# Seven weight-tile subtractions moved from VectorE to GpSimd

## The chip, the core and the metric

The kernel runs on one core of one Trainium2 chip. The metric is the time of one execution on the device in microseconds (us). Engine names in the profile: PE is TensorE (matrix products; PEld its weight loads), DVE is VectorE, ACT is ScalarE, POOL is GpSimd, SP is the engine that issues most transfers.

## The reference

A delta-rule recurrence over 32 heads (4 x 8, 768 steps, head size 48), followed by a two-layer network with a clipped quadratic in the middle:

```python
for t in range(S):
    y[:, :, t] = np.einsum('bhd,bhde->bhe', q[:, :, t], state)
    v_old = np.einsum('bhde,bhd->bhe', state, kt)
    state = state + bt[..., None] * np.einsum('bhd,bhe->bhde', kt, vt - v_old)
...
h = x @ w_in                       # 3072 x 384 @ 384 x 2048
g = np.where(h >= 1, h, np.where(h <= -1, 0, (h + 1) ** 2 / 4))
out = g @ w_out                    # 3072 x 2048 @ 2048 x 384
```

All inputs are fp32.

## The kernel before

**Two computations in one.** The recurrence is done in chunks of 64 steps; two chunks make a group G of 512 rows for the network, six groups in all. For each chunk, Gram matrices are formed on TensorE and triangular systems are solved on VectorE (in the first two groups by L355 and L357, a product and a subtraction per step, called inversion steps here; later by L366 and L368), then merged and applied in a chain of small products.

**The network** runs in items. An item n is one tile f of 128 hidden columns for the rows of one group: `up` (L738, nine products into a PSUM bank h), an activation (L877), the square (L891), the clipping on VectorE (L893, called square(n) in the prediction; it reads h and is what frees it), a rounding to `ghi` on ScalarE (L856) and the rest `glo` on VectorE (L857), and `down` (L753), which follows two items later. There are two h banks, so up(n) waits for L893 of item n - 2. The items of the first group are six of half width, ten of full width (n = 6 to 15, tiles 6 to 15), then the other halves of the first six.

**Numbers in two parts.** Products run on a rounded high half and a low half, in three passes. The network's weights come as 16 tiles, each with both layers' part, as packed integers, and are unpacked once, in the first part of the run, in five steps per tile f:

```python
def grow(f):    # ScalarE, L189
def shift(f):   # VectorE, L195
def join(f):    # VectorE, L201
def cast(f):    # ScalarE, L205: high half, WT[f][:, :, 0, :]
def low(f):     # VectorE, L208: low half, WT[f][:, :, 1, :]
```

Steps on VectorE stand in the fixed order shift(f), join(f), low(f - 1); those on ScalarE in the order grow(f + 2), cast(f). The unpacked numbers lie in `X4` (`xb` in the profile), four slots taken in turn, so grow(f + 4) needs low(f). `up` and `down` of tile f need its low half.

**Order.** Every engine works its instructions in the order in which the program issues them. The order is written out by hand: the strings FILL give, for each item, which steps of unpacking (A for ScalarE, D for VectorE), of the solver, of loads and of masks stand at which place.

**Other work of VectorE around the place of the edit:** the masks of Q (L264, from PSUM), scalings of V (L292), transposes (L394, L396), subtractions from PSUM (L498). GpSimd clears parts of `XT` (L393, L449) there, and later masks Q (L272) and A (L331).

Of the kernel before, what the change touches and what calls it, by code (L numbers as in the profile page):

```python
# [11 lines left out]
ALU = mybir.AluOpType  # L12
# [28 lines left out]
def delta_rule_moe(ctx: ExitStack, tc: tile.TileContext, kqa, kqb, kv, beta, w, out):  # L41
# [14 lines left out]
    nc = tc.nc  # L56
# [14 lines left out]
    K, KE, GE, Q, KV, XB, RAW, WT = {}, {}, {}, {}, {}, {}, {}, {}  # L71
# [112 lines left out]
    X4 = sb.tile([P, 4, 2, DM], F32, name="xb")  # L184
# [20 lines left out]
        nc.scalar.copy(out=WT[f][:, :, 0, :], in_=X4[:, f % 4])  # L205

    def low(f):
        nc.vector.tensor_tensor(out=WT[f][:, :, 1, :], in0=X4[:, f % 4], in1=WT[f][:, :, 0, :], op=ALU.subtract)  # L208

    done = set()  # L210

# [447 lines left out]
    spare += START  # L659
    acts = [(f, grow) for f in range(2)] + [x for f in range(FT) for x in ((f + 2, grow), (f, cast)) if x[0] < FT]  # L660
    vecs = [x for f in range(FT + 1) for x in ((f, shift), (f, join), (f - 1, low)) if 0 <= x[0] < FT]
    sv, ln, raws = [scale_v(g) for g in range(4)], [lanes(0), lanes(1)], []
    tasks = {"A": unpack(acts), "D": unpack(vecs), "B": restore(), "L": ln[1], "s": sv[0], "t": sv[1], "v": sv[2], "z": sv[3]}
# [197 lines left out]
    for n, item in enumerate(items):  # L861
# [9 lines left out]
        if at_ == 2 * HALF:  # L871
            spare.clear()
        assert (item[1], low) in done, item
        h = up(*item)

# [74 lines left out]
```

## Time and profile before

| | |
|---|---|
| median of three runs | 591.88 us (589.80 to 596.24) |
| profiled execution | 590.3 us, of which the span of its instructions 588.6 us |
| busy in the span | PE 97%, PEld 84%, DVE 69%, ACT 56%, POOL 9% |
| granted TensorE clock, mean | 0.992 |

The shares are of the whole span, over stages that differ; the edit touches some 40 us of it.

### The profile page before, as it was taken

What the parts mean: (1) busy time and instruction counts of PE and PEld (TensorE: products, weight loads), DVE (VectorE), ACT (ScalarE), POOL (GpSimd) and SP (SyncE); (2) the same over time, 40 slices, a digit from 0 to 9 for tenths busy, and PEclk for the clock granted to TensorE, in tenths of its full rate; (3) what the DMA queues carried; (4) which work ended last, traced back from release to release, by engine and by line L of the source; (5) the groups of instructions that cost most, each with busy time, mean ns of one, the idle gap of its engine ahead of it and who ended that gap; (6) DMA issues with size and microseconds to landing.
All of it is one profiled execution on the core that took longest, in us unless ns stands there. A gap on an engine that the chain in (4) does not pass through costs nothing.

```text
span 588.6 us, 21697 instructions
## 1 busy us (share of the span) xinstructions
PE 569.0 (97%) x9585; PEld 493.3 (84%) x9585; DVE 405.2 (69%) x828; ACT 327.5 (56%) x587; POOL 54.5 (9%) x91
## 2 busy tenths in 40 slices
PE   8998899999999999999999999999999999999996
PEld 7776788788978888888888888888888888898986
DVE  5977999963689864599954599954599955333332
ACT  4648886358644575545575445575445564454443
POOL 6200010000000500010400011300011300000000
PEclk9979999999999999999999999999999999999999
DMA  5673766200333111134011134011133000020001
GB/s 147 199 253 138 213 212 192 77 4 10 95 81 100 31 32 39 39 97 114 24 33 41 37 103 119 16 30 45 36 106 96 1 3 16 15 55 1 0 2 53
DMA packets 32302, 42.77 MB, mean 73 GB/s; under 512 B 7056, under 2 KB 26768, under 8 KB 32208
## 3 DMA queue, kind: packets, MB, share of 16 engines
q1 hardware_dynamic: 31216, 40.41, 24.0%
q8 instruction: 75, 1.23, 0.9%
q0 software_dynamic: 576, 0.57, 0.4%
q10 hardware_dynamic: 416, 0.39, 0.2%
q14 instruction: 19, 0.16, 0.1%
HBM read 34.47 MB, written 4.72 MB: 67 GB/s over the span
## 4 chain that ended last, share of the span: by engine, by line
PE 47%; issue 22%; DVE 14%; DMA 6%; SPq 6%; ACT 2%; POOL 1%; POOLq 0%; DVEq 0%; ACTq 0%
PE h L738 18%; PE o L753 17%; DMA wt<-in_w_dram 4%; PE ch L534 3%; PE ch L237 2%; DVE s L893 2%; PE ch L508 2%; DVE pr L366 1%; DVE A L368 1%; DVE glo L857 1%; PE ch L250 1%; SPq L595 1%; PE ch L492 1%; DMA KV<-in_kv_dram 1%; DVE wt L208 1%
## 5 line engine op out<-in xcount | busy, mean ns | idle before, releaser
L738 PE MATMUL h<-xb,wt 128*128 128x512 f32 (+1 forms) x918 | 223.0, 386 | 5.1 <-DVE s L893 2.0
L753 PE MATMUL o<-wt,ghi 128*128 128x384 f32 x768 | 200.0, 342 | 0.1
L738 PEld LDWEIGHTS h<-xb,wt 128*128 128x128 f32 x918 | 161.8, 188 | 38.9 <-DVE s L893 3.4
L753 PEld LDWEIGHTS o<-wt,ghi 128*128 128x128 f32 x768 | 137.2, 188 | 7.0 <-issue 0.3
L753 PE MATMUL o<-wt,glo 128*128 128x384 f32 x384 | 129.4, 337 | 0.4 <-DVE glo L857 0.4
L856 ACT CAST ghi<-s 128x512 fp32r<-128x512 f32 (+1 forms) x102 | 60.8, 597 | 120.4 <-DVE s L893 107.8
L893 DVE SCALAR_TENSOR_TENSOR s<-s,h 128x512 f32<-128x512 f32 (+1 forms) x102 | 66.3, 650 | 77.1 <-ACT s L891 76.8
L877 ACT ACTIVATE s<-h,half 128x512 f32<-128x512 f32 (+1 forms) x102 | 67.4, 661 | 53.8 <-PE h L738 53.6
L857 DVE TENSOR_TENSOR glo<-s,ghi 128x512 fp32r<-128x512 f32 (+1 forms) x102 | 66.8, 654 | 39.5 <-ACT ghi L856 39.3
L753 PEld LDWEIGHTS o<-wt,glo 128*128 128x128 f32 x384 | 72.1, 188 | 1.0 <-DVE glo L857 1.0
L891 ACT ACTIVATE s<-s 128x512 f32<-128x512 f32 (+1 forms) x102 | 62.2, 610 | 2.2
L368 DVE TENSOR_TENSOR A<-A,pr 128x30 f32<-128x30 f32 (+14 forms) x120 | 45.4, 378 | 4.4
L366 DVE TENSOR_TENSOR pr<-A 128x30 f32<-128x30 f32 (+14 forms) x120 | 43.4, 362 | 2.2
L272 POOL TENSOR_SCALAR_AFFINE_SELECT Q<-Q 64x512 f32<-64x512 f32 x32 | 21.7, 680 | 117.4 <-ACT Q L260 116.0
L165 PE MATMUL o<-wx 128*128 128x512 f32 x87 | 27.8, 464 | 1.5 <-DVE tiny L175 1.5
L534 PEld LDWEIGHTS ch<-Q,SU 64*64 64x64 f32 (+3 forms) x1056 | 22.4, 135 | 3.7 <-ACT ghi L856 1.5
L534 PE MATMUL ch<-Q,SU 64*64 64x64 f32 (+3 forms) x1056 | 24.7, 222 | 0.0
L331 POOL TENSOR_SCALAR_AFFINE_SELECT A<-A 128x1024 f32<-128x1024 f32 x4 | 5.6, 1390 | 191.5 <-DMA xb<-X 148.1
L165 PEld LDWEIGHTS o<-wx 128*128 128x128 f32 x87 | 18.2, 220 | 5.6 <-DVE tiny L175 1.5
L626 DVE TENSOR_TENSOR SU<-ch,SU 48x384 f32<-48x384 f32 x36 | 19.9, 554 | 3.9 <-PE ch L607 3.5
L590 DVE TENSOR_TENSOR X<-ch,X 128x128 fp32r<-128x128 f32 x20 | 5.8, 292 | 23.5 <-ACT xb L586 22.5
L517 ACT COPY SU<-ch 64x384 f32<-64x384 f32 (+1 forms) x30 | 14.3, 476 | 7.0 <-PE ch L508 6.7
(168 smaller groups left out, 559.5 us busy)
## 6 DMA issues: line engine op xcount, KB each, us to landing
wt<-in_w_dram SPq DMA_DIRECT2D x16, 768.0 KB, 5.6
out_dram<-wx SPq DMA_DIRECT2D x44, 96.0 KB, 2.2
KV<-in_kv_dram SPq DMA_DIRECT2D x36, 96.0 KB, 2.4
KV<-in_kv_dram SPq DMA_DIRECT2D x72, 48.0 KB, 2.3
KV<-in_kv_dram SPq DMA_DIRECT2D x12, 192.0 KB, 2.7
xb<-X SPq DMA_DIRECT2D x60, 32.0 KB, 2.0
K<-in_kqb_dram SPq DMA_DIRECT2D x12, 128.0 KB, 2.6
Q<-in_kqb_dram SPq DMA_DIRECT2D x12, 128.0 KB, 2.7
```

Of the source, the lines that this page charges most:

```text
L165: nc.tensor.matmul(warm_ps, warm[:, 0:P], warm, start=True, stop=True)
L272: nc.gpsimd.affine_select(out=y, in_=y, pattern=[[0, H], [1, C]], base=0, channel_multiplier=-1, compare_op=ALU.is_gt, fill=0.0)
L366: nc.vector.tensor_tensor(out=pr, in0=A[:, 0:n, j:j + 1].broadcast_to([P, n, m]), in1=A[:, j:j + 1, j + 1:32].broadcast_to([P, n, m]), op= ...
L368: nc.vector.tensor_tensor(out=A[:, 0:n, j + 1:32], in0=A[:, 0:n, j + 1:32], in1=pr, op=ALU.add)
L534: nc.tensor.matmul(yy[i][o * C:o * C + C, e, p], SF[rows, u:u + C], w_[rows, x, k, :], **how)
L738: nc.tensor.matmul(h[:, cols(bs)], WT[f][:, 0, x, k * P:(k + 1) * P], XB[G][:, y, k, cols(bs)], start=(n == 0), stop=(n == 8))
L753: nc.tensor.matmul(oacc[G, k], (ghi, glo)[x][:, k * P:(k + 1) * P], WT[f][:, 1, y, :], start=(new and n == 0), stop=(left[G, b] == 0 and n ...
L856: nc.scalar.copy(out=ghi[:, c], in_=s[:, c])
L857: nc.vector.tensor_tensor(out=glo[:, c], in0=s[:, c], in1=ghi[:, c], op=ALU.subtract)
L877: nc.scalar.activation(out=s[:, c], in_=h[:, c], func=AF.Relu, bias=mid, scale=0.5)
L891: nc.scalar.activation(out=s[:, c], in_=s[:, c], func=AF.Square)
L893: nc.vector.scalar_tensor_tensor(out=s[:, c], in0=s[:, c], scalar=1.0, in1=h[:, c], op0=ALU.min, op1=ALU.max)
```

## The change

For tiles 9 to 15 the subtraction low(f) is issued to GpSimd in place of VectorE. Operands, place in the program and everything else stay as they are.

```diff
     def low(f):
-        nc.vector.tensor_tensor(out=WT[f][:, :, 1, :], in0=X4[:, f % 4], in1=WT[f][:, :, 0, :], op=ALU.subtract)
+        (nc.gpsimd if f > 8 else nc.vector).tensor_tensor(out=WT[f][:, :, 1, :], in0=X4[:, f % 4], in1=WT[f][:, :, 0, :], op=ALU.subtract)
```

On GpSimd, in the stretch from the transfers of staged rows (L595) to the clearing of `XT` (L449), the seven subtractions stand as follows (`xb_176` is X4, `wt9` to `wt15` the weight tiles):

```order
 L314 MEMSET X_619 128x16 x2
 L595 DMA xb_865<-wt15_1416 16x2x256 x3
+L208 TENSOR_TENSOR wt9_1617<-xb_176,wt9_1617 128x2x384
+L208 TENSOR_TENSOR wt10_1650<-xb_176,wt10_1650 128x2x384
+L208 TENSOR_TENSOR wt11_1740<-xb_176,wt11_1740 128x2x384
 L393 MEMSET XT_173 128x32x16
+L208 TENSOR_TENSOR wt12_1788<-xb_176,wt12_1788 128x2x384
+L208 TENSOR_TENSOR wt13_1883<-xb_176,wt13_1883 128x2x384
+L208 TENSOR_TENSOR wt14_1993<-xb_176,wt14_1993 128x2x384
+L208 TENSOR_TENSOR wt15_2242<-xb_176,wt15_2242 128x2x384
 L449 MEMSET XT_173 32x16x32 x4
```

The memset of L393 now stands behind three subtractions and those of L449 behind all seven.

On VectorE, where tile 10 is joined and tile 9's low half was made, ahead of two inversion steps:

```order
 L201 SCALAR_TENSOR_TENSOR xb_176<-wt10_1398,xb_176 128x768
 L857 TENSOR_TENSOR glo_1621<-s_1602,ghi_1620 128x512
-L208 TENSOR_TENSOR wt9_1617<-xb_176,wt9_1617 128x2x384
 L355 TENSOR_TENSOR pr_1625<-X_619,A16_712 128x126
 L357 TENSOR_TENSOR X_619<-X_619,pr_1625 128x2x7x9
```

The inversion steps follow `glo` at once.

On VectorE, where tile 13 is joined and tile 12's low half was made, ahead of tile 14's shift and join:

```order
 L201 SCALAR_TENSOR_TENSOR xb_176<-wt13_1555,xb_176 128x768
 L893 SCALAR_TENSOR_TENSOR s_1821<-s_1821,h_1811 128x512
-L208 TENSOR_TENSOR wt12_1788<-xb_176,wt12_1788 128x2x384
 L195 TENSOR_SCALAR xb_176<-xb_176 128x768
 L201 SCALAR_TENSOR_TENSOR xb_176<-wt14_1615,xb_176 128x768
```

Shift and join of tile 14 follow the clipping at once. TensorE, ScalarE and SP have the same instructions in the same order as before.

## Rows read from the trace of the kernel before

**Rows 1.** Page, part 1: busy us, share of span, instructions.

```profile
PE 569.0 (97%) x9585; PEld 493.3 (84%) x9585; DVE 405.2 (69%) x828; ACT 327.5 (56%) x587; POOL 54.5 (9%) x91
```

**Rows 2.** Windows: busy us by engine, clock, DMA share, GB/s.

```profile
88.00:116.30 28.30, 26.26 (x609) 22.28 (x608) 27.75 (x54) 14.20 (x22) 0.50 (x1) 1.00 0.47 139
...
127.10:588.60 461.50, 453.79 (x6819) 398.19 (x6818) 296.60 (x602) 249.45 (x451) 36.67 (x50) 1.00 0.18 47
```

**Rows 3.** Waits of PE and PEld, 76 to 131: total, times, longest.

```profile
PE h L738 <- DVE s L893: 2.0, 3, 1.1
...
PEld h L738 <- DVE wt L208: 0.6, 1, 0.6
...
PEld o L753 <- DVE glo L857: 0.3, 1, 0.3
```

**Rows 4.** Timeline of DVE, 70 to 132: start, us, instruction.

```profile
85.10 0.68 DVE L893 SCALAR_TENSOR_TENSOR s<-s,h 128x512 f32<-128x512 f32 x1
85.70 0.95 DVE L201 SCALAR_TENSOR_TENSOR xb<-wt,xb 128x768 int32<-128x768 int32 x1
...
87.17 0.95 DVE L208 TENSOR_TENSOR wt<-xb,wt 128x768 fp32r<-128x768 f32 x1
88.03 0.29 DVE L355 TENSOR_TENSOR pr<-X,A 128x126 f32<-128x126 f32 x1
...
92.15 2.09 DVE L264 TENSOR_TENSOR Q<-ch,mask 64x512 f32<-64x512 f32 x3
...
101.51 0.22 DVE L355 TENSOR_TENSOR pr<-X,A 128x56 f32<-128x56 f32 x1
...
109.36 0.96 DVE L201 SCALAR_TENSOR_TENSOR xb<-wt,xb 128x768 int32<-128x768 int32 x1
...
110.69 1.22 DVE L394 STREAM_TRANSPOSE XT<-A 128x512 f32<-128x512 f32 x1
111.81 0.64 DVE L857 TENSOR_TENSOR glo<-s,ghi 128x512 fp32r<-128x512 f32 x1
```

**Rows 5.** Timeline of ACT, 70 to 132: casts of tiles 9 and 10.

```profile
84.47 0.83 ACT L205 CAST wt<-xb 128x768 fp32r<-128x768 f32 x1
...
88.45 0.82 ACT L205 CAST wt<-xb 128x768 fp32r<-128x768 f32 x1
```

**Rows 6.** Timeline of POOL, whole span (idle before, releaser in brackets).

```profile
3.83 0.81 POOL L148 TENSOR_SCALAR_AFFINE_SELECT perm<-perm 128x32 f32<-128x32 f32 x3
...
115.80 1.09 POOL L449 MEMSET XT<- 32x512 f32 x2 [36.29 <-PE ch L419]
...
164.50 1.26 POOL L331 TENSOR_SCALAR_AFFINE_SELECT A<-A 128x1024 f32<-128x1024 f32 x1 [43.45 <-PE ch L607]
...
191.18 3.12 POOL L272 TENSOR_SCALAR_AFFINE_SELECT Q<-Q 64x512 f32<-64x512 f32 x4 [25.19 <-ACT Q L260]
...
285.99 2.89 POOL L272 TENSOR_SCALAR_AFFINE_SELECT Q<-Q 64x512 f32<-64x512 f32 x4 [4.69 <-ACT Q L260]
```

**Rows 7.** Timeline of DVE beside two of these maskings.

```profile
192.86 0.68 DVE L893 SCALAR_TENSOR_TENSOR s<-s,h 128x512 f32<-128x512 f32 x1
...
286.82 0.68 DVE L368 TENSOR_TENSOR A<-A,pr 128x58 f32<-128x58 f32 x1
...
288.23 0.71 DVE L368 TENSOR_TENSOR A<-A,pr 128x30 f32<-128x30 f32 x1
```

**Rows 8.** Timeline of DVE, 254 to 256.5, GpSimd idle.

```profile
255.68 0.19 DVE L368 TENSOR_TENSOR A<-A,pr 128x30 f32<-128x30 f32 x1
...
256.15 0.22 DVE L368 TENSOR_TENSOR A<-A,pr 128x58 f32<-128x58 f32 x1
```

**Rows 9.** Timeline of PE, 70 to 140: a merge, up(13), a chain product.

```profile
114.44 1.26 PE L419 MATMUL ch<-A,XT 32*32 32x16 f32 x128
...
116.35 2.36 PE L738 MATMUL h<-xb,wt 128*128 128x512 f32 x9 [0.65 <-DVE s L893]
...
136.90 1.36 PE L508 MATMUL ch<-KV,XT 64*64 64x48 f32 x64
```

## Prediction

> **What bounds the kernel now.** I read the busy shares first, then windows by stretch, the waits of TensorE, and last the timelines of VectorE, ScalarE and GpSimd where the seven subtractions lie. VectorE is busy for 405.2 us of the span and GpSimd for 54.5 [rows 1]; as averages these two shares invite the move. They hide that the edit touches one stretch only. From 88.0 to 116.3 us VectorE is busy for 27.75 of 28.30 us and TensorE is the engine with holes, 26.26 us; from 127.1 us to the end TensorE is busy for 453.79 of 461.50 us and VectorE for little more than half [rows 2]. In the first of these stretches TensorE's waits are VectorE's doing: 2.0 us in three waits of `up` for the L893 that frees its h bank, 0.6 us of a weight load for a low half itself (L208), 0.3 us for a `glo` [rows 3]. Together 2.9 us: no relief of VectorE can give back more than about that. One of the three waits stands ahead of `up(13)`, 0.65 us [rows 9].
>
> Names below: low(f), join(f) (L201), shift(f) (L195) and cast(f) (L205) are the steps of tile f; glo(n) (L857), square(n) (L893), up(n) and down(n) belong to item n. In the stretch of the edit item n uses tile n.
>
> **What leaves VectorE.** Seven subtractions of 0.95 us; the next instruction starts 0.87 us after one (88.03 after 87.17) [rows 4], so 7 x 0.87 = 6.1 us. Of these, five (tiles 9 to 13) lie ahead of square(11), the last that TensorE waits for; the other two lie where VectorE already idles for ScalarE, so they are worth nothing on the path. Without any other effect, 5 x 0.87 = 4.4 us earlier at square(11) is more than TensorE can take: the three waits for L893 go whole, 2.0 us, and of the 0.9 us for a low half and a `glo` about half, which overlaps them. I count 2.4 us; then there is no gap left.
>
> **What it costs on GpSimd.** No two-input operation of GpSimd is in the trace, so its length is bounded by rows. The one-input select on 128x1024 took 1.26 us and three on 128x32 took 0.81, or 0.27 each [rows 6]: 1.0 ns per element over 0.27, hence 1.04 us for 768 elements if a second input were free. If it costs as much as the first, 0.27 + 2 x 0.77 = 1.81 us. The dearest row per element is the masking of Q, 3.12 us for four of 512, 1.5 ns per element, which doubled gives 2.3 us. I take 1.8 us, since the 128x1024 row is the nearest in partitions and length; the ends are 1.04 and 2.3.
>
> GpSimd itself has room: each tile's subtraction becomes ready with its cast on ScalarE, 84.47 to 85.30 us for tile 9 [rows 5], where VectorE came to it only at 87.17. So the low halves are finished no later than before, and the 0.6 us weight-load wait goes. Two sorts of GpSimd memsets now stand behind subtractions in its queue. The one of L393 comes behind low(11), about 95 us, and the first product that reads its zeros (L419) runs from 114.44 [rows 9]. The four of L449, which began at 115.80 [rows 6], come behind low(15), about 125 us; four of some 0.55 us end near 128, ahead of the product L508 at 136.90 [rows 9]. Both cost nothing while GpSimd keeps within some 8 us of that.
>
> **The lock.** The decisive row is what happens to VectorE beside GpSimd. While GpSimd masked Q (four selects in 2.89 us, 0.72 each) [rows 6], VectorE's inversion steps of 58 and 30 elements (L368), with both inputs in SBUF, took 0.68 and 0.71 us [rows 7]; the same shapes alone took 0.22 and 0.19 [rows 8]. Each waited about 0.5 us, until GpSimd's instruction was nearly through. An L893 in the middle of such a masking (192.86, within 191.18 to 194.30), with one input in PSUM, took 0.68, no more than elsewhere [rows 4, 6, 7]. So VectorE stands still for about the length of a GpSimd instruction less 0.2, whenever its next instruction has two SBUF inputs, and goes on where one input is PSUM. In SBUF - State Buffer, section "Who interferes with whom", the Trainium skill gives this as an exclusive lock, taken by a VectorE instruction with two SBUF inputs or in a two-port mode against a GpSimd one that reads SBUF; the trace agrees.
>
> Shift(f) has its one input and its output in SBUF, and no row shows one beside GpSimd; I take it as held, and where it is not the waits of low(10) and low(13) below are 0.3 us shorter each. Joins, inversion steps (L355, L357), `glo` and scalings of V are of the held kind by rows 7; the squares, the masks of Q from PSUM (2.09 us at 92.15), the transposes (L394) and the subtractions from PSUM are not. I price the hold at 1.7 us: 1.81, less 0.2, plus some 0.1 for starting again.
>
> **Following the order with a hold of 1.7 us.**
> - low(9): cast(9) is done at 85.30, VectorE is in square(6) from 85.10 [rows 4, 5]. GpSimd starts at about 85.37, and join(10), due at 85.70, waits until 87.07: 1.37 us.
> - low(10): cast(10) ends near 89.2 [rows 5], VectorE is in shift(11), whose end near 89.54 lets GpSimd in until 91.24. Square(7) runs beside it for 0.60, then join(11) waits 1.10 us.
> - low(11): it gets in as the mask of Q begins (2.0 us from PSUM), and is through when that is: 0.
> - low(12): inversion steps and scalings follow without a gap (L355 at 101.51 is one) [rows 4]: the whole 1.70 us.
> - low(13): shift(14) ends, join(14) (109.36) waits 1.70 us.
> - low(14): the transpose L394 (110.69) covers part; glo(10) (111.81) waits 1.03 us.
>
> Together 6.9 us of waits ahead of glo(10). Taken away ahead of it are four subtractions, 3.5 us. So glo(10) ends 3.4 us later, and down(10), which waited for it by 0.3 us already, stands 3.3 us later. Square(11) comes behind low(13) too, so it is 3.4 - 0.9 = 2.5 us later. TensorE loses the 0.65 us gap that it had ahead of up(13): 3.3 - 0.65 = **2.6 us later**. From there VectorE is ahead again, and the rest of the run is TensorE's at 98% busy, with nothing in it that takes 2.6 us back. low(15) falls where VectorE waits for ScalarE.
>
> **Sum.** The profiled execution took 590.3 us (588.6 span, 1.7 around it); 590.3 + 2.6 = 592.9. The median of the three runs is 591.9, 1.6 above it; on that the forecast is **594.5 us**, plus 0.4%.
>
> **Rivals.**
> 1. No hold: VectorE and GpSimd run side by side in this pairing. Then the 2.4 us above are gained: 591.9 - 2.4 = 589.5. For it: holds are seen with selects and with products only. Against: the held rows have two inputs in SBUF, as the joins have, and the new instruction reads twice what a select reads.
> 2. Slower by a cascade: the GpSimd instruction holds for 1.9 us or more. From about 1.85 the order turns: low(10) is ready before VectorE has begun shift(11) and holds that too, join(11) and cast(11) come later, low(11) misses the cover of the mask multiplication, and shift(12) waits for it. At 1.9 the same following gives 4.9 us at up(13), at 2.3 it gives 7.3: 596.8 to 599.2. For it: 1.81 is only 0.1 off that point. Against: the waits in rows 7 were shorter than the GpSimd instruction, not longer.
> 3. The second input is nearly free: a hold of 1.04 us. The waits ahead of square(11) are then 3.9 us against 4.4 removed; the time stays within 0.5 us of 591.9. For it: the 1.0 ns per element of L331. Against: it would have to read two tensors at the pace of one.
>
> GPSIMD Engine Reference of the Trainium skill, section "Performance versus the Vector engine", gives 4497 ns for a two-input add of 2048 elements, as an estimate 1.7 us pro rata for 768; no run here shows it, and the sum by it would be the forecast. By its advice to keep elementwise work on VectorE the sign would be the forecast's too.
>
> That the edit does not do what it says can be left out: the order shows seven instructions gone from VectorE and seven on GpSimd, and nothing else moved.
>
> **How the numbers follow.** Forecast, hold between 1.4 and 1.85 us (1.2 to 3.2 us slower): 0.55. Rival 2: 0.25. Rival 1: 0.12. Rival 3: 0.08. About 1% (5.9 us) is what a measurement of this kernel can tell from no change. Only the dearer half of rival 2 is beyond it, holds over some 2.1 us, 0.16, with 0.03 for a hold priced wrongly in kind: slower 0.19. Faster by 1% is not to be had from 2.9 us of waits: 0.03. Within: 0.78. The range reaches from rival 1, 589.0, to rival 2's end, 599.5.
>
> **What would show it.** In the changed kernel's timeline GpSimd has seven L208 of 1.7 to 2.0 us, the first near 85.4. VectorE's join(10), join(11), an inversion step near 101, join(14) and glo(10) are 1 to 1.7 us longer than alone, squares and the masks from PSUM keep theirs. VectorE's busy time hardly falls, since waits count as busy. TensorE's wait ahead of up(10) grows, down(10) waits some 3 us for `glo`, and up(13) starts near 119 in place of 116.35. I am wrong if joins keep 0.95 us beside a GpSimd L208 (rival 1), if those last over 2 us or under 1.3, if VectorE gets in front of a waiting GpSimd instruction so that low(12) comes late for up(12), or if a later stage takes the delay back.

## The result and the profile after

The changed kernel takes 594.89 us (median of 20 runs, 591.95 to 599.18), the kernel before 590.93 us (20 runs, 588.79 to 596.24). The ratio of the runs is 1.0063, 95% interval 1.0044 to 1.0081: by it the change costs 3.7 us, 2.6 to 4.8. The profiled execution took 594.9 us, its span 593.2.

The page's first part [rows 1] reads now:

```profile
PE 571.5 (96%) x9585; PEld 495.0 (83%) x9585; DVE 405.8 (68%) x821; ACT 328.3 (55%) x587; POOL 67.7 (11%) x98
```

VectorE has seven instructions less and is busy for as long as before; GpSimd has 13.2 us more. The windows around the edit [rows 2]:

```profile
88.00:119.00 31.00, 25.90 (x508) 22.19 (x503) 29.77 (x49) 14.14 (x24) 9.97 (x6) 0.94 0.40 120
119.00:130.00 11.00, 11.00 (x350) 9.18 (x340) 6.85 (x12) 4.71 (x9) 3.94 (x5) 1.00 0.06 14
130.00:593.00 463.00, 454.13 (x6825) 398.32 (x6819) 296.27 (x602) 250.13 (x451) 36.75 (x50) 1.00 0.18 47
```

TensorE has some 5 us of holes between 88 and 119 us, where it had 2 in the 28 us from 88 to 116.3, and the last number but two, its granted clock, is 0.94 there. GpSimd's timeline shows the seven subtractions (start, us, what ended the idle time before):

```profile
84.26 1.85 POOL L208 TENSOR_TENSOR wt<-xb,wt 128x768 fp32r<-128x768 f32 x1 [6.44 <-ACT wt L205]
88.19 2.05 POOL L208 TENSOR_TENSOR wt<-xb,wt 128x768 fp32r<-128x768 f32 x1 [2.09 <-PE ch L250]
92.55 1.87 POOL L208 TENSOR_TENSOR wt<-xb,wt 128x768 fp32r<-128x768 f32 x1 [2.32 <-ACT wt L205]
94.36 0.53 POOL L393 MEMSET XT<- 128x512 f32 x1
99.97 1.92 POOL L208 TENSOR_TENSOR wt<-xb,wt 128x768 fp32r<-128x768 f32 x1 [5.08 <-ACT wt L205]
108.85 1.85 POOL L208 TENSOR_TENSOR wt<-xb,wt 128x768 fp32r<-128x768 f32 x1 [6.96 <-ACT wt L205]
112.46 1.81 POOL L208 TENSOR_TENSOR wt<-xb,wt 128x768 fp32r<-128x768 f32 x1 [1.76 <-ACT wt L205]
123.36 1.86 POOL L208 TENSOR_TENSOR wt<-xb,wt 128x768 fp32r<-128x768 f32 x1 [9.09 <-ACT wt L205]
125.29 2.24 POOL L449 MEMSET XT<- 32x512 f32 x4
```

And VectorE's timeline, the instructions that lay beside them [rows 4]:

```profile
83.94 0.68 DVE L893 SCALAR_TENSOR_TENSOR s<-s,h 128x512 f32<-128x512 f32 x1
84.53 2.39 DVE L201 SCALAR_TENSOR_TENSOR xb<-wt,xb 128x768 int32<-128x768 int32 x1
...
89.03 2.02 DVE L201 SCALAR_TENSOR_TENSOR xb<-wt,xb 128x768 int32<-128x768 int32 x1
...
92.63 2.09 DVE L264 TENSOR_TENSOR Q<-ch,mask 64x512 f32<-64x512 f32 x3
94.63 0.67 DVE L195 TENSOR_SCALAR xb<-xb 128x768 int32<-128x768 int32 x1
...
100.20 1.78 DVE L357 TENSOR_TENSOR X<-X,pr 128x78 f32<-128x78 f32 x1
...
109.01 2.51 DVE L201 SCALAR_TENSOR_TENSOR xb<-wt,xb 128x768 int32<-128x768 int32 x1
...
113.01 1.81 DVE L857 TENSOR_TENSOR glo<-s,ghi 128x512 fp32r<-128x512 f32 x1
```

Two more lengths of the kernel before, from its timeline of VectorE (a shift and an inversion step of 78 elements):

```profile
88.56 0.55 DVE L195 TENSOR_SCALAR xb<-xb 128x768 int32<-128x768 int32 x1
...
101.23 0.24 DVE L357 TENSOR_TENSOR X<-X,pr 128x78 f32<-128x78 f32 x1
```

The joins take 2.39, 2.02 and 2.51 us in place of 0.95 or 0.96, the inversion step 1.78 in place of 0.24, the `glo` of item 10 1.81 in place of 0.64. Their waits add up to 1.44 + 1.07 + 1.54 + 1.55 + 1.17 = 6.8 us, 6.9 with 0.12 us of shift(12), which took 0.67 beside the memset of L393. Squares and the mask of Q keep their length beside the same GpSimd instructions.

TensorE's timeline from down(10) to up(13) [rows 9], and its clock in windows:

```profile
112.04 0.62 PE L753 MATMUL o<-wt,ghi 128*128 128x384 f32 x2
114.88 0.45 PE L753 MATMUL o<-wt,glo 128*128 128x384 f32 x1 [2.21 <-DVE glo L857]
115.16 0.73 PE L753 MATMUL o<-wt,ghi 128*128 128x384 f32 x2
...
118.06 1.49 PE L419 MATMUL ch<-A,XT 32*32 32x16 f32 x128
```

```profile
114.00:116.00 2.00, 1.12 (x4) 1.12 (x5) 2.00 (x3) 0.00 (x0) 0.28 (x1) 0.82 0.00 0
116.00:118.00 2.00, 2.00 (x7) 1.63 (x6) 1.76 (x3) 0.17 (x1) 0.00 (x0) 0.50 0.32 97
118.00:120.00 2.00, 2.00 (x131) 1.87 (x131) 0.83 (x2) 1.83 (x4) 0.00 (x0) 0.83 0.51 121
```

TensorE stands for 2.21 us for glo(10), and right behind it its granted clock is 0.50, half of 2.4 GHz, for some 3.4 us.

Executions differ by some microseconds ahead of this place: square(6) starts at 85.10 before and at 83.94 after, though no instruction ahead of it was changed. So the stretch from the start of square(6) to the start of up(15) is the measure of the edit in a trace. It is 45.82 us before (130.92 less 85.10) and 50.10 after (134.04 less 83.94): 4.28 us longer. From TensorE's timelines, before and then after:

```profile
130.92 2.37 PE L738 MATMUL h<-xb,wt 128*128 128x512 f32 x9
```

```profile
134.04 2.36 PE L738 MATMUL h<-xb,wt 128*128 128x512 f32 x9
```

### The profile page after: what moved, and what is told of

It reads as the page before. It is cut to its first block, busy times and chain, and to the rows that moved or that the text cites. A ratio compares the mean times of both kernels' runs of the same rounds, so it can differ in the third digit from the quotient of the medians.

```text
span 593.2 us, 21710 instructions
## 1 busy us (share of the span) xinstructions
PE 571.5 (96%) x9585; PEld 495.0 (83%) x9585; DVE 405.8 (68%) x821; ACT 328.3 (55%) x587; POOL 67.7 (11%) x98
## 4 chain that ended last, share of the span: by engine, by line
PE 49%; issue 22%; DVE 13%; DMA 7%; SPq 4%; ACT 3%; POOL 1%; POOLq 0%; DVEq 0%; ACTq 0%
PE h L738 19%; PE o L753 17%; DMA wt<-in_w_dram 4%; PE ch L534 3%; PE ch L237 2%; PE ch L508 1%; DVE glo L857 1%; DVE xb L201 1%; DVE A L368 1%; DVE pr L366 1%; PE ch L250 1%; DVE s L893 1%; PE ch L492 1%; DMA xb<-X 1%; DMA KV<-in_kv_dram 1%
## 5 line engine op out<-in xcount | busy, mean ns | idle before, releaser
L165 PE MATMUL o<-wx 128*128 128x512 f32 x87 | 29.0, 479 | 1.5 <-DVE tiny L175 1.5
L201 DVE SCALAR_TENSOR_TENSOR xb<-wt,xb 128x768 int32<-128x768 int32 x16 | 19.3, 1206 | 0.1
```

The source lines that it names most:

```text
L165: nc.tensor.matmul(warm_ps, warm[:, 0:P], warm, start=True, stop=True)
L201: nc.vector.scalar_tensor_tensor(out=x, in0=RAW.pop(f).bitcast(I32)[:, :, 0::2], scalar=29, in1=x, op0=ALU.logical_shift_right, op1=ALU.bi ...
```

## The experiments

Theory 1 is that of the forecast: a GpSimd instruction that reads SBUF holds any VectorE instruction with two inputs there. Theory 2: VectorE is not held, TensorE waits for late low halves. Theory 3: any GpSimd work beside VectorE slows it. Experiments 1 to 6 are edits of `low(f)` of the kernel before, 9 of that and of one memset; 7 and 8 start from the changed kernel. L208 stays L208 in all of them.

| kernel | ratio to before, 95% interval | square(6) to up(15), us | against before |
|---|---|---|---|
| before | 1 | 45.82 | |
| changed | 1.0063 (1.0044 to 1.0081) | 50.10 | +4.28 |
| 1 memset in place | 0.9957 (0.9929 to 0.9985) | 42.94 | -2.88 |
| 2 subtraction in addition | 1.0157 (1.0118 to 1.0196) | 54.52 | +8.70 |
| 3 memsets in addition | 1.0033 (1.0003 to 1.0064) | 46.74 | +0.92 |
| 4 tiles 13, 14 | 1.0102 (1.0053 to 1.0150) | 51.11 | +5.29 |
| 5 tiles 9 to 12 | 1.0044 (1.0007 to 1.0082) | 47.92 | +2.10 |
| 6 tiles 10, 12, covered | 0.9998 (0.9966 to 1.0030) | 44.55 | -1.27 |
| 7 changed, wait filled | 1.0087 (1.0057 to 1.0118) | 49.50 | +3.68 |
| 8 changed again | 1.0090 (1.0053 to 1.0128) | 48.04 | +2.22 |
| 9 covered, memset ahead | 0.9980 (0.9948 to 1.0011) | 43.85 | -1.97 |

The stretch is one execution each; the ratios rest on 4 to 20 runs of the kernel in the row.

**1. An instruction that only writes, in place of the subtraction.**

```diff
-        nc.vector.tensor_tensor(out=WT[f][:, :, 1, :], ...)
+        nc.gpsimd.memset(WT[f].bitcast(F32)[:, :, 1, :], 0.0) if f > 8 else nc.vector.tensor_tensor(...)
```

> For tiles 9 to 15 GpSimd fills the low half with zeros in place of subtracting: an instruction that only writes. The low halves of these seven tiles are left out, all else is as in the changed kernel. Theory 1 (VectorE is held by a GpSimd instruction that reads SBUF, whenever its own has two inputs there): the joins keep 0.95 us, VectorE is relieved of seven subtractions and nothing is charged, so 2.0 to 2.4 us faster than before, ratio 0.996. Theory 2 (the loss comes from late low halves, VectorE itself is not held): also faster, since zeros come early, but then the wait ahead of down(10) in the changed kernel would have to be for a low half. Theory 3 (any GpSimd work beside VectorE slows it): no gain, ratio 1.000 or above.

Measured: 0.9957, the stretch 2.88 us shorter. The gain that the forecast gave to a world without holds is there as soon as GpSimd reads nothing. VectorE's own subtraction in this kernel, beside the first memset (84.41 to 85.15 us on GpSimd), and an inversion step of 126 elements beside the second (87.72 to 88.46) take what they take in the kernel before [rows 4]:

```profile
84.72 0.95 DVE L208 TENSOR_TENSOR wt<-xb,wt 128x768 fp32r<-128x768 f32 x1
...
88.13 0.28 DVE L355 TENSOR_TENSOR pr<-X,A 128x126 f32<-128x126 f32 x1
```

Theory 3 falls here for work with two inputs. Theory 2 has no support in the changed kernel's trace, where nothing waits for a low half.

**2. The subtraction in addition.**

```diff
+    scratch = sb.tile([P, 2, DM], F32, name="wx")
     def low(f):
         nc.vector.tensor_tensor(out=WT[f][:, :, 1, :], ...)
+        f > 8 and nc.gpsimd.tensor_tensor(out=scratch, in0=X4[:, f % 4], in1=WT[f][:, :, 0, :], op=ALU.subtract)
```

> VectorE makes all low halves as before; GpSimd does the seven subtractions in addition, into a tile that nobody reads. Theory 1: the waits of the changed kernel without its relief, so glo(10) and square(11) are some 7 to 8 us late: 6.5 to 9 us slower than before, ratio 1.011 to 1.015. Theory 2 (late low halves): the low halves come from VectorE at their old place, so no change, ratio 1.000. Theory 3: as theory 1.

Measured: 1.0157, a little above the range, which its interval covers; the stretch is 8.70 us longer. No low half that is used comes from GpSimd here, so theory 2 falls; holds without relief cost about what theory 1 said: glo(10) ends 8.25 us later, counted from square(6), where 7 to 8 were expected. VectorE's timeline:

```profile
87.92 2.41 DVE L201 SCALAR_TENSOR_TENSOR xb<-wt,xb 128x768 int32<-128x768 int32 x1
...
91.72 1.93 DVE L355 TENSOR_TENSOR pr<-X,A 128x126 f32<-128x126 f32 x1
...
99.49 1.67 DVE L208 TENSOR_TENSOR wt<-xb,wt 128x768 fp32r<-128x768 f32 x1
```

A join, an inversion step and VectorE's own subtraction wait 1.46, 1.64 and 0.72 us; with a scaling of V, join(14) and glo(10), not shown here, it is 8.2 us. GpSimd can wait as well: its fifth subtraction here is recorded for 2.63 us, behind a subtraction and a shift of VectorE.

**3. Memsets in addition.** After each cast GpSimd copies one element and clears the unused tile three times, 2.3 us.

```diff
+        f > 8 and [nc.gpsimd.tensor_copy(out=scratch[:, 0, 0:1], in_=WT[f][:, 0, 0, 0:1])] + [nc.gpsimd.memset(scratch, 0.0) for _ in range(3)]
```

> VectorE makes all low halves as before; for each of tiles 9 to 15 GpSimd, after the cast, copies one element and then clears a tile that nobody reads three times, over 2 us of writing. Theory 1: instructions that only write do not hold two-input work; the fast one-input shift may be held for one memset (0.7 us) now and then; within 1 us of before, ratio 0.999 to 1.002. Theory 2: 1.000. Theory 3 (any GpSimd work slows VectorE): like the extra subtractions, 1.01 or more.

Measured: 1.0033 with an interval that begins at 1.0003, so the ratio is above the expected 0.999 to 1.002, which the interval reaches into; the stretch is 0.92 us longer, within what was expected. GpSimd's and then VectorE's timeline show both halves of the answer:

```profile
95.68 2.33 POOL L208 MEMSET wx<- 128x768 f32 x3
```

```profile
96.39 0.95 DVE L208 TENSOR_TENSOR wt<-xb,wt 128x768 fp32r<-128x768 f32 x1
97.25 1.17 DVE L195 TENSOR_SCALAR xb<-xb 128x768 int32<-128x768 int32 x1
```

The two-input subtraction beside three memsets keeps 0.95 us; the shift, with one input, takes 1.17 in place of 0.55. So reading is what holds two-input work, and writing is enough to hold the shift. The interval, 0.2 to 3.8 us, holds the 0.92 us of the stretch; whether more is lost outside it was not followed up.

**4. Tiles 13 and 14 alone.**

```diff
+        (nc.gpsimd if f in (13, 14) else nc.vector).tensor_tensor(...)
```

> Only tiles 13 and 14 are subtracted by GpSimd. Theory 1: the waits of join(14) and glo(10) stay, 2.7 us together, and nothing has been taken away ahead of glo(10): 2.1 to 3.5 us slower than before, the upper end if TensorE's granted clock falls after its wait as it did in the changed kernel (0.94 between 88 and 119 us). So two of seven moves would bear most of the loss. Theory 2 (late low halves): low(13) and low(14) are wanted only at 116 and 123 us, ready by 112 and 115, so no change, ratio 1.000.

Measured: 1.0102, 6.0 us (3.1 to 8.9), where 2.1 to 3.5 were expected. The intervals of this kernel and of all seven moves overlap, so that two moves cost more than seven is not shown; that they can bear most of the loss is. The holds are as expected, but for the shift that is held in join(14)'s place: VectorE's shift(14) and glo(10) take

```profile
110.66 2.21 DVE L195 TENSOR_SCALAR xb<-xb 128x768 int32<-128x768 int32 x1
...
115.33 1.83 DVE L857 TENSOR_TENSOR glo<-s,ghi 128x512 fp32r<-128x512 f32 x1
```

or 1.66 and 1.19 us more than alone, and glo(10) ends 2.8 us later, counted from square(6). This is also the row that the prediction lacked: a subtracting GpSimd holds a shift. The rest goes with TensorE's clock, in its timeline and windows:

```profile
117.22 0.69 PE L753 MATMUL o<-wt,glo 128*128 128x384 f32 x1 [2.78 <-DVE glo L857]
...
122.55 4.10 PE L738 MATMUL h<-xb,wt 128*128 128x512 f32 x9
```

```profile
116.00:118.00 2.00, 0.78 (x2) 0.79 (x3) 2.00 (x2) 0.00 (x0) 0.61 (x1) 0.54 0.00 0
118.00:126.00 8.00, 8.00 (x145) 6.85 (x145) 5.09 (x9) 2.61 (x5) 1.04 (x2) 0.50 0.20 55
```

For about 10 us, from within the wait on, it has the lower of its two levels, and up(13) takes 4.10 us in place of 2.36.

**5. Tiles 9 to 12.**

```diff
+        (nc.gpsimd if 9 <= f <= 12 else nc.vector).tensor_tensor(...)
```

> Only tiles 9 to 12 are subtracted by GpSimd. Theory 1 (a hold of VectorE by a reading GpSimd instruction): join(10), join(11) and an inversion step near 101 wait 1.4, 1.1 and 1.5 us, low(11) is covered by the mask of Q; 4.0 us of waits against 3.5 taken away, so glo(10) 0.6 us late and TensorE 0.5 to 1.0 us late at up(15), with no wait of 2 us and the clock at full speed throughout: ratio 1.000 to 1.003. If the loss were spread over the moves evenly, four sevenths of the changed kernel's: 1.004.

Measured: 1.0044 with an interval that holds both 1.003 and the 1.004 of an even spread, so the ratio does not tell them apart. The trace does: glo(10) ends 0.67 us later, counted from square(6), where 0.6 was expected and four sevenths of the changed kernel's 3.5 would be 2.0. The stretch is 2.10 us longer, not 0.5 to 1.0. Part of it goes with the clock: after a wait of 1.79 us ahead of up(10) it falls, and up(10) takes 3.53 us in place of 2.33; the changed kernel with 1.89 us at the same place does not show that. Another 0.85 us is lost between up(13) and up(14), where TensorE has pauses of 0.42 and 0.22 us that the profile puts down to nothing.

```profile
96.47 3.53 PE L738 MATMUL h<-xb,wt 128*128 128x512 f32 x9 [1.79 <-DVE s L893]
```

**6. Two moves under cover.** Tiles 10 and 12, each started behind the VectorE step after which two microseconds of untouched work begin.

```diff
+        (f in (10, 12) and nc.gpsimd.tensor_copy(out=scratch[:, 0, 0:1], in_=S["X"][:, 0, 0, 15:16] if f == 10 else S["X32"][:, 16, 16:17])); (nc.gpsimd if f in (10, 12) else nc.vector).tensor_tensor(...)
```

> Only tiles 10 and 12 are subtracted by GpSimd, and each waits (by a copy of one element) for the VectorE step ahead of a stretch that reads PSUM or has one input: the mask of Q (2.0 us) for tile 10, a transpose and two subtractions (2.05 us) for tile 12. Theory 1: each hold of 1.7 us lies beside work that it does not touch, so VectorE is relieved of 1.7 us ahead of square(10) and waits for 0.3 us at most: from square(6) to up(15) 1.2 to 1.9 us less than before, ratio 0.997 to 0.998, faster than both kernels. Any theory in which moving a subtraction costs as such (late low halves, any work of GpSimd): 1.001 or above.

Measured: the stretch is 1.27 us shorter, in the expected range; the ratio, 0.9998, is between the two cases and tells neither. GpSimd's and VectorE's timelines at tile 10:

```profile
92.89 1.85 POOL L208 TENSOR_TENSOR wt<-xb,wt 128x768 fp32r<-128x768 f32 x1
94.69 0.51 POOL L393 MEMSET XT<- 128x512 f32 x1
```

```profile
92.60 2.09 DVE L264 TENSOR_TENSOR Q<-ch,mask 64x512 f32<-64x512 f32 x3
94.61 1.02 DVE L195 TENSOR_SCALAR xb<-xb 128x768 int32<-128x768 int32 x1
```

The subtraction is hidden whole beside the mask. What is left is the memset of L393, which now stands behind it and meets shift(12): 1.02 us in place of 0.55. The prediction had put this memset's move at nothing.

**7. The wait filled.** All seven moved, and 20 unused products ahead of down(10):

```diff
+        [nc.tensor.matmul(bank[:, 256:512], warm[:, 0:P], warm[:, 0:256], start=True, stop=True) for _ in range(more)]
...
+ a=lambda g: merge16_a(g % 2, 20 * (g == 3))
```

> The changed kernel, all seven moved, with 20 products of 128x256 into an unused half of a PSUM bank issued ahead of down(10), so that TensorE works through most of its wait for glo(10). Their results are not used. If the lower clock after that wait (0.5 for 3.4 us) is a consequence of TensorE standing still there, the clock stays at full speed and the stretch from square(6) to up(15) is 2.6 to 3.2 us longer than before in place of 4.3: ratio 1.004 to 1.005. If the clock has another cause, it falls at the same place and the stretch stays at 4.3 or above.

Measured: the clock stays at 1.00 from 112 to 128 us, and up(13) comes 2.80 us later than before, counted from square(6), against 4.29 in the changed kernel. But the ratio is 1.0087, no better than the changed kernel's, and the stretch is 3.68 us longer, since later TensorE stood still for 1.37 us in down(11) for nothing that the profile shows (the first line is up(13)):

```profile
119.17 2.36 PE L738 MATMUL h<-xb,wt 128*128 128x512 f32 x9
...
125.16 0.45 PE L753 MATMUL o<-wt,glo 128*128 128x384 f32 x1 [1.37 <-issue]
```

Over the whole span its runs have nearly the clock of the kernel before (mean 0.989 against 0.991), so little of its loss is the clock's; whether the pause is in every run is not shown.

**8. The changed kernel again.**

> The changed kernel once more, beside the others on one chip: ratio 1.004 to 1.008, the stretch from square(6) to up(15) 4 us longer than before, with one stretch of half clock behind the wait of down(10).

Measured: 1.0090, above the expected range, which its interval (1.0053 to 1.0128) reaches into. glo(10) ends 30.79 us after square(6), against 30.88 in the first execution and 27.35 before: the holds repeat to 0.1 us. The half clock lies elsewhere:

```profile
113.10 3.36 PE L738 MATMUL h<-xb,wt 128*128 128x512 f32 x9 [0.67 <-DVE s L893]
...
119.43 0.45 PE L753 MATMUL o<-wt,glo 128*128 128x384 f32 x1 [0.81 <-DVE glo L857]
...
122.56 2.36 PE L738 MATMUL h<-xb,wt 128*128 128x512 f32 x9
```

It begins in up(12), behind a wait of 0.67 us, and ends ahead of down(10). There it is hidden, since down(10) waits for glo(10) anyway, now for 0.81 us in place of 2.21. Behind that wait the clock is whole, and up(13) (the last line) starts 2.72 us later than before, counted from square(6); the stretch is 2.22 us longer, not 4. The expectation missed that.

**9. Covered, with the memset ahead.**

```diff
+        (f == 10 and nc.gpsimd.memset(ZT[:, :, :, 16:32], 0.0)); ...
-            if G and s:
+            if G and s and G > 1:
```

> As the covered kernel (tiles 10 and 12 on GpSimd, each started where VectorE reads PSUM), with the memset of L393 issued ahead of the first of the two instead of behind it, so that it runs near 79 us, as before the change, and no longer meets shift(12). Theory 1: shift(12) goes back from 1.02 to 0.55 us, and the stretch from square(6) to up(15) is 1.5 to 2.0 us shorter than before (1.3 in the covered kernel). Ratio 0.997, which 5 rounds with an interval of 0.3% may not tell from 1; the stretch in the trace decides. If shift(12) keeps 1.0 us, it was not the memset that held it.

Measured: shift(12) is back at

```profile
95.61 0.56 DVE L195 TENSOR_SCALAR xb<-xb 128x768 int32<-128x768 int32 x1
```

and the stretch is 1.97 us shorter than before, as expected. The ratio is 0.9980 with an interval that still holds 1: faster than the changed kernel, and than the kernel before by this stretch of the trace; the timed ratio does not settle the second.

## Why the prediction was right

**The bound.** Seen rightly: VectorE bounds this stretch, and what it loses TensorE loses.

**The length on GpSimd.** 1.8 us was taken; the seven took 1.81 to 2.05, and the two longest, 1.92 and 2.05, began while VectorE was still in an inversion step and in a shift. The length agrees with the guess that the second input costs as much as the first; one size does not show that this is the reason. The pro-rata estimate from GPSIMD Engine Reference of the Trainium skill, "Performance versus the Vector engine", 1.7 us, is 0.1 short.

**The holds.** Waits of 1.37, 1.10, 0, 1.70, 1.70 and 1.03 us were worked out, 6.9 in all; 1.44, 1.07, 0.12, 1.54, 1.55 and 1.17 were measured, 6.9 in all. They fell on the instructions named, and low(11) was covered by the mask. glo(10) was to be 3.4 us late and is 3.5 us late from square(6). Down(10) was to wait some 3 us and waited 2.21, since TensorE came to it later, after longer waits ahead of up(10) (1.89 us for 1.05) and up(12) (0.67 for 0.25). What SBUF - State Buffer of the Trainium skill says in "Who interferes with whom" agrees with these runs in both directions: two-input work is held by a GpSimd instruction that reads (experiment 2: 1.5 us) and not by one that only writes (experiments 1 and 3: 0.28 and 0.95 us as alone).

**The shift.** Taken as held, without a row; experiment 4 shows it, 2.21 us in place of 0.55.

**What left VectorE.** 2.4 us were to be gained without holds; experiment 1 shows 2.88 in the stretch and 2.5 by the ratio.

**The rivals.** No hold: excluded by the waits above. A hold of 1.9 us: undisturbed the instruction took 1.81 to 1.87, and VectorE goes on about 0.14 us before GpSimd's recorded end (the join held from 84.53 ends at 86.92, its own 0.95 us after 85.97; GpSimd's instruction ends at 86.11), so the hold is some 1.7 us and the cascade did not set in. A nearly free second input: excluded by 1.81 us.

**What was left out.** The step from holds to TensorE, 3.3 - 0.65 = 2.6 us, counted a gap at its length (and took 3.3 where glo(10) is 3.4 late; a wait that was there already takes nothing off). It can have a price behind it: in the first execution after, the products of down(10) behind the wait and the next merge ran at half clock and took 1.5 us longer than before, so up(13) is 4.3 us late from square(6), not 2.6. Where the clock is whole between the wait and up(13) it is 2.8 (experiment 7) and 2.7 (experiment 8, the same program as the changed kernel), near the 2.6. So the holds were sized rightly and a term for the clock was missing; at up(13) it is worth 1.7 us in one execution of the changed kernel and 0.1 in the other, and in experiment 4 some 3 us of the stretch (5.29, where 2.81 - 0.65 would be 2.2).

The timed runs agree. Each has its mean granted clock on record; one straight line for each kernel, both of the same slope, through the times of experiment 8 and of the kernel before beside it (10 and 34 runs, 3.8 us for 0.01 of the clock) puts them 2.9 us apart at equal clock, 95% interval 1.9 to 3.9. Their means as they stand are 5.1 us apart, at clocks of 0.985 and 0.991. This is an estimate, and it does not tell in which stretch the clock fell.

The forecast of a 0.44% loss stands against 0.63% (0.44 to 0.81), so it is at the lower end of what was measured. That the time itself, 594.5 us, is within 0.4 us of the measured 594.89 is in part luck: the forecast started from a median of 591.88 us of three runs where twenty give 590.93, and this excess made up for most of the missing term.

**The rest of the run.** That nothing later takes the delay back was right: from the start of up(15) to the end it is 457.7 us before, 459.2 and 457.9 in the two executions after.

**The memsets.** "Cost nothing" was right for L449 and wrong by 0.12 us for L393 in the changed kernel, 0.5 in experiment 6.

**What stays open.** Which wait of TensorE is followed by a fall of the clock: 1.89 us ahead of up(10) was not in one execution, 1.79 us at the same place was in another, and 0.67 us ahead of up(12) in a third. Whether the fall in a given run is caused by the wait nearest to it is argued and not shown. Experiment 7 is on its side, but it is one execution, and experiment 8 lacks the fall behind down(10) without any filling, its wait there being 0.81 us. The pauses of TensorE that the profile puts down to nothing (1.37 us in experiment 7) are unexplained too.

## What to carry to other kernels

Moving a two-input elementwise step from a busy VectorE to an idle GpSimd doubled its length here (0.95 to 1.85 us) and did not take it off VectorE. In these runs it paid only where it ran beside VectorE work that reads PSUM or transposes, as in experiment 6 (a shift with one input is held too, experiment 4): count what VectorE will run beside it, not GpSimd's idle share. If such work exists, tie the start of the GpSimd instruction to it, and look at what then stands behind it in GpSimd's queue. A new gap on TensorE of one or two microseconds may cost more than its length through the granted clock.

## What the runs showed of the hardware that was not expected

- GpSimd's memsets, which read nothing, leave two-input VectorE work alone but hold the fast shift (one input, SBUF to SBUF, 0.55 us for 768 elements): 1.17 us in experiment 3, 1.02 in experiment 6, and 0.56 again once the memset was moved.
- The same program has stretches of half clock of differing number and place. Between 40 and 80 us, ahead of the edit, the mean granted clock was 0.96 in one execution of the changed kernel and 0.80 in another:

```profile
40.00:80.00 40.00, 36.43 (x1025) 30.49 (x1020) 32.92 (x67) 34.12 (x63) 1.54 (x3) 0.96 0.51 157
```

```profile
40.00:80.00 40.00, 37.28 (x1012) 32.08 (x1007) 28.64 (x57) 29.99 (x56) 0.00 (x0) 0.80 0.45 146
```

Square(6) began at 83.94 us in the first (first fence) and at 88.59 in the second. That is as much as the whole effect of the change, and a reason to measure an edit within its stretch.
